# Loading one pair in bf16 on another queue, holding the next one back, and reordering the first stages of a fused attention and gated feed-forward kernel

## The chip, the cores and the metric

The kernel runs on one core of a Trainium2 chip. A core has a matrix engine (TensorE, PE in the profile, with its weight loads as PEld), VectorE (DVE), ScalarE (ACT), GpSimd (POOL) and SyncE (SP). SP, ScalarE and GpSimd can also issue DMAs. The time is the device time of one execution in microseconds; a kernel is judged by the median of several executions. The profile comes from one of them.

## The reference

The first half is attention with a relative position bias in the manner of T5, for 8 batches of 8 heads, 576 positions and a head size of 64. The second half is a bilinear feed-forward layer on the 4608 rows that come out.

```python
scores = scale * np.matmul(q, k.transpose(0, 1, 3, 2))
bias = bias_table[bucket]                     # bucket depends on |i - j| alone
scores = scores + bias.transpose(2, 0, 1)[None, :, :, :]
scores = scores - np.max(scores, axis=-1, keepdims=True)
attn = np.exp(scores)
attn = attn / (np.sum(attn, axis=-1, keepdims=True) + 1e-09)
attn_out = np.matmul(attn, v)                 # (8, 8, 576, 64)
...
x = attn_out.transpose(0, 2, 1, 3).reshape(B * S, H * D)
a = x @ w_a                                   # 512 -> 1536
b = x @ w_b
out = (a * b) @ w_out                         # 1536 -> 512
```

All inputs and the output are float32 in DRAM; the weights are 512 x 1536 (twice) and 1536 x 512.

## The kernel before

**Pairs.** Two heads of one batch make a pair; pair p is heads 2(p mod 4) and the next of batch p div 4, so there are 32 pairs, and pairs 0 to 3 are batch 0. Of the 576 positions 512 are the main part (four blocks of 128) and 64 are the tail. For each pair TensorE needs q and k with the head size on the partitions: `QT` and `KT`, two buffers each, which also hold the transposed tails. The names of the steps are those of small functions. `qk1(p, t)` makes the scores of key block t, `ex` is ScalarE's exponential, `mul` is VectorE's product with the exponential of the bias (`W_sb[p % 4]`, a band around the diagonal), `qk_tail`, `ex_tail` and `mul_tail` do the same for what touches the tails (with `Wt_sb`), `av(p, jq)` multiplies with v for query block jq, `norm` divides by the row sums and writes `XG`, and `t_x` turns `XG` into the feed-forward input `xn_sb`, by a DMA transpose on SP for most pairs, or on TensorE with a copy `c_x` for pairs 2 and 3.

**Loads.** q, k and v are read in rows of 64 floats (256 bytes). Loads issued on GpSimd cast to bf16 as they move (`load_p`, `load_t`, `load_vp`, `load_tails`, `load_vt`); loads on SP and ScalarE keep float32 (`load32`, into `q32`, `k32` and, for the tails of batch 0, `qt32`, `kt32`). Before the change all four pairs of batch 0 come in float32 on SP, with k of pair 0 on ScalarE, and are turned by float32 transposes (`t32`, against `id32`). From batch 1 on, q and k come through GpSimd into `qn`, `kn` (two buffers, by batch), v into `vm` (main) and `vt` (tails), the tails of q and k into `qtl`, `ktl` (a buffer for two batches). Pairs 4 to 11 are turned on TensorE in bf16 (`t_q`, `t_k`, with `c_q`, `c_k` as copies out of PSUM), later ones by DMA transposes.

**The bias table.** A small float32 matmul with a one-hot matrix makes the 8 x 256 table, ScalarE takes its exponential, and it goes out to a DRAM tensor `tab`. The bands `W_sb` and `Wt_sb` are read back from it with overlapping rows (`load_w`, and the loop over hh at L225), on GpSimd. `warm_up(n)` puts n products of zeros on TensorE before and after the table's matmul.

**Order.** Every engine's order is that of the program text; nothing is scheduled by a planner. So is the order of each DMA queue. On GpSimd, eight semaphores go round over its DMAs, so an issue waits until the one eight places before it has landed; SP's and ScalarE's DMAs share another eight. After the start, GpSimd's order is: W of pair 0, Wt, v of pair 0 and its tails, W of pair 1, the rest of v of batch 0, W of pair 2, q and k of pair 4, W of pair 3, the tails of batch 1, the first third of w_a and w_b, v of pair 4, the tails of v of batch 1, the rest of q and k of batch 1, the second third of w_a and w_b, the rest of v of batch 1, the last third, then q and k of batch 2, w_out (`wo_sb`), memsets of the second tail buffers, and the tails of q and k of batches 2 and 3.

**Stages.** A loop over s = 0, 1, 2 does pairs 0 to 2 with `q_next`, `k_next` and `tails_next` for the pair after; straight code does pair 3 and begins pair 4 and the feed-forward. From s = 4 on each stage does one pair and between its steps puts feed-forward units (`U`): for each chunk of 512 rows 12 units `ff_a` (x @ w_a, `pa`, copied to `ha`), 12 `ff_b` (`pb`, whose product with `ha` is `g`), and 12 thirds of `ff_o` (`po`, g @ w_out). The first chunk's 24 units of a and b are used up in stage s = 7, where the first `ff_o` stands on TensorE just behind `t_k(8)`, the transposes of k of pair 8 with its tails.

```python
        for mc in range(m0, m1):
            nc.tensor.matmul(out=ff[key][:, :], lhsT=w[df // FW][:, mc, 128 * (df % FW):128 * (df % FW) + 128],
                             rhs=xn_sb[mc][:, xin(c)],
                             start=(mc == 0), stop=(mc == NMC - 1))
```

`xn_sb[mc]` is filled by pair mc of the batch, so the first unit of each kind is begun with mc 0 to 2 and ended with mc 3 (`m0 = 3`) once pair 3 is there.

Of the kernel before, what the change touches and what calls it, by code (L numbers as in the profile page):

```python
# [13 lines left out]
def kernel(  # L14
# [11 lines left out]
    nc = tc.nc  # L26
    FP32 = mybir.dt.float32
    BF16 = mybir.dt.bfloat16
# [6 lines left out]
    SM = 128 * NM  # L35
# [6 lines left out]
    NMC = DM // 128  # L42
# [107 lines left out]
    def load_tails(b, nb):  # L150
        load_pad(nc.gpsimd, k, ktl[b // 2 % 2], b, nb)
        load_pad(nc.gpsimd, q, qtl[b // 2 % 2], b, nb)

    def load_vt(b, nb):
        load_pad(nc.gpsimd, v, vt[b // 2 % 2], b, nb)

    def load_w_in(part):
        for src, dst in ((moe_w_a, wa_sb), (moe_w_b, wb_sb)):
            nc.gpsimd.dma_start(
                out=dst[part][:, :, :],  # L160
                in_=src[:, WC * part:WC * part + WC].rearrange("(m p) n -> p m n", p=128))

    def load_w_out():
        nc.gpsimd.dma_start(out=wo_sb[:, :, :], in_=moe_w_out.rearrange("(t p) n -> p t n", p=128))

    def load_w(eng, hp):
        eng.dma_start(out=W_sb[hp][:, :, :],
                      in_=bass.AP(tensor=tab, offset=2 * hp * TB, ap=[[1, 128], [TB, 2], [1, 384]]))
# [12 lines left out]
    def load32(p, src, out, engs):  # L181
        for h in range(2):
            load_h(engs[h], src, out[:, p, :, h, :], 0, 2 * p + h)
# [18 lines left out]
    ones(nc.gpsimd, vt[0])  # L202
    for x in (ktl, qtl):
        pad(nc.gpsimd, x[0], Dh)
    for p in (2, 3):
        load32(p, q, q32, (nc.sync, nc.sync))
        load32(p, k, k32, (nc.sync, nc.sync))

    warm = ps_ff.tile([128, 512], FP32, tag="ffn", name="warm")

    def warm_up(n):
        for _ in range(n):
            nc.tensor.matmul(out=warm[:, :], lhsT=zero_sb[:, 0:128], rhs=zero_sb[:, :],
                             start=True, stop=True)
# [2 lines left out]
    tps = ps_av.tile([128, 512], FP32, tag="av", name="tab_ps")  # L217
    nc.tensor.matmul(out=tps[0:H, 0:NR], lhsT=bt_sb[0:NB, :], rhs=oh_sb[0:NB, :],
                     start=True, stop=True)
    warm_up(5)  # L220
    nc.scalar.activation(out=tab_sb[0:H, 127:127 + NR], in_=tps[0:H, 0:NR], func=ACTF.Exp)
    nc.scalar.dma_start(out=tab.ap(), in_=tab_sb[0:H, :])

    load_w(nc.gpsimd, 0)
    for hh in range(2):  # L225
        nc.gpsimd.dma_start(out=Wt_sb[64 * hh:64 * hh + 64, :, :],
                            in_=bass.AP(tensor=tab, offset=hh * TB + 192,
                                        ap=[[1, 64], [2 * TB, H // 2], [1, 192]]))
    load_vp(0, 0)
    load_vt(0, 1)  # L230
    load_w(nc.gpsimd, 1)
    load_t(v, None, 0, 2, 8)
    load_w(nc.gpsimd, 2)
    load_p(q, qn, 1, 0)
    load_p(k, kn, 1, 0)
    load_w(nc.gpsimd, 3)
    load_tails(1, 1)
    load_w_in(0)
    load_vp(1, 0)
    load_vt(1, 1)  # L240
    load_t(q, qn, 1, 2, 8)
    load_t(k, kn, 1, 2, 8)
    load_w_in(1)
# [4 lines left out]
    def copy(eng, out, in_):  # L248
        if eng is nc.scalar:
            nc.scalar.activation(out=out, in_=in_, func=ACTF.Copy)  # L250
        else:
            nc.vector.tensor_copy(out=out, in_=in_)
# [21 lines left out]
    def bank(where, dt, name):  # L274
        return where[0].tile([128, 512 if dt is FP32 else 1024], dt, tag=where[1], name=name)
# [212 lines left out]
    def ff_bank(name):  # L488
# [4 lines left out]
            where = TR if turn3 % 3 == 0 else FF  # L493
        return where[0].tile([128, 512], FP32, tag=where[1], name=name)

    def ff_mm(c, df, w, key, m0, m1):
        if m0 == 0:
            ff[key] = ff_bank(f"{key}{c}_{df}")
        for mc in range(m0, m1):
            nc.tensor.matmul(out=ff[key][:, :], lhsT=w[df // FW][:, mc, 128 * (df % FW):128 * (df % FW) + 128],  # L500
                             rhs=xn_sb[mc][:, xin(c)],
                             start=(mc == 0), stop=(mc == NMC - 1))

    def ff_a(c, df, m0=0):
        ff_mm(c, df, wa_sb, "pa", m0, NMC)
# [26 lines left out]
    units = []  # L532
    for c in range(NCH):
        for df in range(NDF):
            m0 = 3 if c == 0 and df == 0 else 0
            units.append(lambda c=c, df=df, m0=m0: ff_a(c, df, m0))
            units.append(lambda c=c, df=df, m0=m0: ff_b(c, df, m0))
        for tt in range(4):
            for part in range(3):
                units.append(lambda c=c, tt=tt, part=part: ff_o(c, tt, part))  # L540
# [9 lines left out]
    def t32(ps, src, p, t):  # L550
        nc.tensor.transpose(ps[:, 128 * t:128 * t + 128], src[:, p, t, :, :], id32[:, :])
# [13 lines left out]
    qk1(0, 1)  # L565

    def q_next(s):
        ps = bank(TR, FP32, f"trq{s + 1}")
        for t in range(NM):
            t32(ps, q32, s + 1, t)  # L570
        copy(None, QT[(s + 1) % 2][:, :], ps[:, :])

    def k_next(s):
        ps = bank(FF, FP32, f"trk{s + 1}")
        for t in range(NM):
            t32(ps, k32, s + 1, t)
        copy(None, KT[(s + 1) % 2][:, 0:SM], ps[:, :])

    def tails_next(p0, n, eng):
        ps = bank(FF, FP32, f"trt{p0}")  # L580
# [6 lines left out]
    for s in range(3):  # L587
        ex(s, 0)
        if s > 0:
            mul(s - 1, 3)  # L590
            mul_tail(s - 1)
        q_next(s)
        qk1(s, 2)
        ex(s, 1)
        k_next(s)
        qk1(s, 3)
        ex(s, 2)
        if s == 0:
            tails_next(0, 2, None)
        else:  # L600
            tails_next(s + 1, 1, ACT)
        if s > 0:
            av(s - 1, 0)
            av(s - 1, 1)
        qk_tail(s)
        mul(s, 0)
        mul(s, 1)
        ex(s, 3)
        if s > 0:
            av(s - 1, 2)  # L610
            norm(s - 1, 0)
            av(s - 1, 3, FF)
        qk1(s + 1, 0)
        ex_tail(s)
        if s > 0:
            av(s - 1, 4)
        mul(s, 2)
        if s > 0:
            norm(s - 1, 3)
            t_x(s - 1)  # L620
        qk1(s + 1, 1)

    load_w_in(2)
    load_t(q, qn, 2, 0, 8)
    load_t(k, kn, 2, 0, 8)
    load_w_out()
    pad(nc.gpsimd, vt[1], Dh + 1)
    ones(nc.gpsimd, vt[1])
    for x in (ktl, qtl):
        pad(nc.gpsimd, x[1], Dh)  # L630
    load_tails(2, 2)

    ex(3, 0)
    mul(2, 3)
# [18 lines left out]
    av_part(3, 0)  # L653
    c_x(2)
    t_q(4, FF)
    c_q(4)
    t_k(4, FF)
    c_k(4)
    qk1(4, 0)
    mul(3, 2)  # L660
    ex(4, 0)
# [2 lines left out]
    av_part(3, 2)  # L664
    av_part(3, None)
    mul(3, 3)
    qk1(4, 1)
    av_part(3, 3)
    ff_mm(0, 0, wa_sb, "pa", 0, 3)
    norm(3, 0)  # L670
    ex(4, 1)
    norm(3, 3)
    t_x(3, AV, range(3))
    ff_mm(0, 0, wb_sb, "pb", 0, 3)
    qk1(4, 2)
    t_x(3, AV, range(3, 5))
    ex(4, 2)
    c_x(3)
    qk1(4, 3)
# [101 lines left out]
```

## Time and profile before

| | us |
|---|---|
| median of 4 runs (lowest, highest) | 436.61 (435.23, 437.3) |
| profiled execution, its own time | 435.23 |
| its span | 433.4 |
| TensorE busy in the span | 413.7 (95%) |
| ScalarE, VectorE, GpSimd busy | 241.8, 196.9, 116.2 |
| mean granted clock of TensorE | 0.987 |

The span runs from the first to the last instruction of the profiled execution; 1.8 us of its time lie around it. A busy TensorE is not one at its peak, since matmuls are pipelined. Times on the timeline count from the span's start. A line of the timeline has the start, the duration, the engine, the line of the kernel, the operation, the tiles written and read, the shape, the number of instructions merged and, in brackets, how long the engine stood idle before and what ended that. A DMA issue on GpSimd shows the time of issuing, not of moving; the list of DMA issues has the time from issue to landing. "DMA share" is the mean busy share of the 16 DMA engines; it goes over 1 where several packets are under way in one engine.

### The profile page before, as it was taken

The numbers are of one execution on the slowest core, as the hardware profiler recorded it, in microseconds if no ns is written. First come the engines' busy times: TensorE is split into PE (matmuls) and PEld (weight loads), VectorE is DVE, ScalarE is ACT, GpSimd is POOL, SyncE is SP. The second block draws the span as 40 slices with busy tenths as digits, with TensorE's granted clock in tenths as the row PEclk, the third lists the DMA queues.
The fourth block names the chain that finished last, engine by engine and source line by source line (L and its number), as shares of the span: only waits on it lengthen the run. The fifth ranks groups of instructions, "written<-read, shape, count | busy, mean of one in ns | idle before, by whom it ended". The sixth has DMA issues, their size and how long they took to land.

```text
span 433.4 us, 8391 instructions
## 1 busy us (share of the span) xinstructions
PE 413.7 (95%) x3365; PEld 203.6 (47%) x3365; DVE 196.9 (45%) x474; ACT 241.8 (56%) x341; POOL 116.2 (27%) x155
## 2 busy tenths in 40 slices
PE   8697997699999999999999999999999999999995
PEld 3464553255444444444444444444444454444442
DVE  3585664145663455335542555355524550430330
ACT  3695566266665666666656666566657642323321
POOL 5895756830626400560037002100000000000000
PEclk9899999699999999999999999999999999999999
DMA  8999999997999990699339920931021012002004
GB/s 161 185 145 129 168 169 188 139 141 172 82 93 76 200 145 15 48 190 156 54 29 188 176 41 8 185 82 39 15 86 39 15 17 81 17 2 97 2 0 97
DMA packets 168279, 41.93 MB, mean 97 GB/s; under 512 B 158728, under 2 KB 163408, under 8 KB 168240
## 3 DMA queue, kind: packets, MB, share of 16 engines
q0 software_dynamic: 108400, 18.69, 60.9%
q1 hardware_dynamic: 58576, 22.38, 27.1%
q8 instruction: 26, 0.43, 0.4%
q10 hardware_dynamic: 1264, 0.34, 0.4%
q14 instruction: 13, 0.11, 0.1%
HBM read 38.80 MB, written 9.45 MB: 111 GB/s over the span
## 4 chain that ended last, share of the span: by engine, by line
PE 80%; DMA 13%; POOL 4%; issue 1%; ACTq 0%; DVE 0%; ACT 0%
PE po L519 22%; PE pa L500 20%; PE pb L500 19%; PE av L404 7%; PE qk L334 6%; DMA vm<-in_v_dram 4%; DMA qn<-in_q_dram 3%; PE av L395 3%; DMA qtl<-in_q_dram 2%; DMA wa<-in_moe_w_a_dram 2%; PE qkt L359 1%; PE qkt L362 1%; DMA k<-in_k_dram 1%; DMA bias_tab<-tab_sb 1%; POOL kn L124 1%
## 5 line engine op out<-in xcount | busy, mean ns | idle before, releaser
L345 ACT ACTIVATE at<-qk 128x1024 bf16<-128x1024 f32 x128 | 126.3, 1025 | 26.4 <-PE qk L334 26.4
L512 DVE TENSOR_TENSOR g<-pb,ha 128x512 bf16<-128x512 f32 x108 | 74.7, 692 | 114.4 <-PE pb L500 96.0
L500 PE MATMUL pa<-xn,wa 128*128 128x512 bf16 x432 | 111.4, 379 | 1.3 <-DMA xn<-XG 0.8
L500 PE MATMUL pb<-xn,wb 128*128 128x512 bf16 x432 | 111.2, 379 | 0.0
L519 PE MATMUL po<-wo,g 128*128 128x512 bf16 x432 | 103.8, 383 | 0.0
L507 ACT ACTIVATE ha<-pa 128x512 f32<-128x512 f32 x108 | 64.6, 598 | 67.5 <-PE pa L500 67.5
L353 DVE TENSOR_TENSOR at<-at,W 128x512 bf16<-128x512 bf16 (+1 forms) x128 | 60.1, 483 | 11.7 <-ACT at L345 8.4
L500 PEld LDWEIGHTS <-wa 128*128 128x128 bf16 x432 | 38.9, 98 | 49.6 <-issue 10.0
L523 ACT ACTIVATE ob<-po 128x512 f32<-128x512 f32 x36 | 21.5, 597 | 70.3 <-PE po L519 70.3
L519 PEld LDWEIGHTS <-g 128*128 128x128 bf16 x432 | 38.9, 99 | 46.4 <-issue 8.5
L500 PEld LDWEIGHTS <-wb 128*128 128x128 bf16 x432 | 39.0, 98 | 45.2 <-issue 5.6
L124 POOL DMA_DIRECT2D vm<-in_v_dram x32 | 27.8, 891 | 108.8 <-PE av L404 102.5
L404 PE MATMUL av<-vm,at 128*128 128x65 bf16 x992 | 44.8, 195 | 0.0
L404 PEld LDWEIGHTS <-at 128*128 128x128 bf16 x992 | 40.6, 99 | 4.1
L440 DVE RECIPROCAL rc<-av 128x6 f32<-128x6 f32 x64 | 12.1, 188 | 59.9 <-PE av L404 57.6
L395 PE MATMUL av<-vt,att 128*128 128x130 bf16 x156 | 35.2, 226 | 2.4 <-DMA vt<-in_v_dram 2.0
L373 ACT ACTIVATE att<-qkt 128x1024 bf16<-128x1024 f32 x32 | 32.7, 1022 | 0.0
L441 DVE TENSOR_TENSOR XG<-av,rc 128x384 bf16<-128x384 f32 x64 | 31.4, 491 | 2.2
L124 POOL DMA_DIRECT2D qn<-in_q_dram x28 | 24.7, 918 | 25.6 <-PE trq L286 19.2
L124 POOL DMA_DIRECT2D kn<-in_k_dram x28 | 24.7, 917 | 7.7 <-DMA vt<-in_v_dram 2.9
L334 PE MATMUL qk<-QTb,KTb 64*128 64x512 bf16 x160 | 24.2, 381 | 0.0
L395 PEld LDWEIGHTS <-att 128*128 128x128 bf16 x156 | 15.4, 98 | 18.0 <-DVE XG L441 10.7
(105 smaller groups left out, 229.2 us busy)
## 6 DMA issues: line engine op xcount, KB each, us to landing
out_dram<-ob SPq DMA_DIRECT2D x32, 256.0 KB, 3.1
qn<-in_q_dram POOLq DMA_DIRECT2D x24, 128.0 KB, 8.5
kn<-in_k_dram POOLq DMA_DIRECT2D x24, 128.0 KB, 11.8
vm<-in_v_dram POOLq DMA_DIRECT2D x24, 128.0 KB, 5.7
wa<-in_moe_w_a_dram POOLq DMA_DIRECT2D x3, 512.0 KB, 6.8
wb<-in_moe_w_b_dram POOLq DMA_DIRECT2D x3, 512.0 KB, 9.6
wo<-in_moe_w_out_dram POOLq DMA_DIRECT2D x1, 1536.0 KB, 14.5
q<-in_q_dram SPq DMA_DIRECT2D x8, 128.0 KB, 3.7
```

Source lines behind the costliest of these rows:

```text
L124: nc.gpsimd.dma_start(out=(vm[b % 2][:, h0:h1, t, 0:Dh] if dst is None else dst[b % 2][:, :].rearrange("p (t h d) -> p t h d", h=H, t=NM)[ ...
L334: nc.tensor.matmul(out=ps[:, hh, :], lhsT=kT_(p, t)[r, :], rhs=qT[r, :, :], start=True, stop=True)
L345: nc.scalar.activation(out=at[:, :, :], in_=ps[:, :, :], func=ACTF.Exp, scale=scale)
L353: nc.vector.tensor_tensor(out=at[:, :, lo:hi], in0=at[:, :, lo:hi], in1=w[:, :, y:(None if z < 0 else z):-1], op=MULT)
L373: nc.scalar.activation(out=at[:, 0:1024].rearrange("p (a x) -> p a x", a=2), in_=ps[:, :, :], func=ACTF.Exp, scale=scale)
L395: nc.tensor.matmul(out=pav[:, slot, :, :], lhsT=x, rhs=vt[b // 2 % 2][:, 4 * i + hp, :, 0:Dh + 1], start=fresh, stop=True, skip_group_chec ...
L404: nc.tensor.matmul(out=pav[:, slot, hh, :], lhsT=x, rhs=vm[i][:, 2 * hp + hh, t, 0:Dh + 1], start=False, stop=True, skip_group_check=True)
L441: nc.vector.tensor_tensor(out=xg[:, j0:j0 + n, :, :], in0=pav[:, 0:n, :, 0:Dh], in1=rc.unsqueeze(3).to_broadcast([128, n, 2, Dh]), op=MULT)
L500: nc.tensor.matmul(out=ff[key][:, :], lhsT=w[df // FW][:, mc, 128 * (df % FW):128 * (df % FW) + 128], rhs=xn_sb[mc][:, xin(c)], start=(mc ...
L507: nc.scalar.activation(out=ha[:, :], in_=ff["pa"][:, :], func=ACTF.Copy)
L512: nc.vector.tensor_tensor(out=g_sb[df][:, :], in0=ff["pb"][:, :], in1=ff["ha"][:, :], op=MULT)
L519: nc.tensor.matmul(out=po[:, :], lhsT=g_sb[df][:, 128 * tt:128 * tt + 128], rhs=wo_sb[:, df, :], start=(df == 0), stop=(df == NDF - 1))
```

## The change

- Pair 2's q and k no longer come in float32 on SP but by `load_p` into `qn[0]` and `kn[0]`, in bf16, on GpSimd, at the place where SP's loads of pairs 2 and 3 stood in the text. That is before the first `load_w` in GpSimd's order. `q_next` and `k_next` turn them in bf16 for s = 1.
- Pair 3's four float32 loads stay on SP but are written down inside stage s = 0, and two one-element memsets on VectorE, behind `mul(0, 0)`, write into the same buffers first, so the loads wait for these.
- `Wt` is loaded on SP instead of GpSimd. The second `warm_up` has 2 products instead of 5.
- The tails of v of batches 0 and 1 are loaded together. The tails of q and k of batch 1 go behind the first third of w_a and w_b.
- The memsets and the tails of q and k of batches 2 and 3 go ahead of q and k of batch 2 and of w_out.
- In the stages s = 1 and 2, `qk_tail(s)` and `mul(s, 0)` go ahead of `av(s - 1, 0)`; `av(s - 1, 2)` and `norm(s - 1, 0)` come ahead of `mul(s, 1)`, and `norm(s - 1, 3)` and `t_x(s - 1)` ahead of `mul(s, 2)`.
- Pair 4's copies out of PSUM move to ScalarE, both behind both transposes. `av_part(3, 3)` goes ahead of `qk1(4, 1)`.
- The feed-forward sums run over mc in the order 0, 2, 1, 3, and the first units are begun with two terms instead of three; the second of them a little later.

```diff
-    for p in (2, 3):
-        load32(p, q, q32, (nc.sync, nc.sync))
-        load32(p, k, k32, (nc.sync, nc.sync))
+    load_p(q, qn, 0, 2)
+    load_p(k, kn, 0, 2)
...
-    warm_up(5)
+    warm_up(2)
     nc.scalar.activation(out=tab_sb[0:H, 127:127 + NR], in_=tps[0:H, 0:NR], func=ACTF.Exp)
     nc.scalar.dma_start(out=tab.ap(), in_=tab_sb[0:H, :])
 
     load_w(nc.gpsimd, 0)
     for hh in range(2):
-        nc.gpsimd.dma_start(out=Wt_sb[64 * hh:64 * hh + 64, :, :],
+        nc.sync.dma_start(out=Wt_sb[64 * hh:64 * hh + 64, :, :],
...
     load_vp(0, 0)
-    load_vt(0, 1)
+    load_vt(0, 2)
...
     load_w(nc.gpsimd, 3)
+    load_w_in(0)
     load_tails(1, 1)
-    load_w_in(0)
     load_vp(1, 0)
-    load_vt(1, 1)
...
+    MC = (0, 2, 1, 3)
+
...
-        for mc in range(m0, m1):
+        for i in range(m0, m1):
+            mc = MC[i]
...
-                             start=(mc == 0), stop=(mc == NMC - 1))
+                             start=(i == 0), stop=(i == NMC - 1))
...
-            m0 = 3 if c == 0 and df == 0 else 0
+            m0 = 2 if c == 0 and df == 0 else 0
...
     def q_next(s):
-        ps = bank(TR, FP32, f"trq{s + 1}")
+        ps = bank(TR, BF16 if s == 1 else FP32, f"trq{s + 1}")
         for t in range(NM):
-            t32(ps, q32, s + 1, t)
-        copy(None, QT[(s + 1) % 2][:, :], ps[:, :])
+            if s == 1:
+                nc.tensor.transpose(ps[:, 128 * t:128 * t + 128], blocks(qn, 2)[:, t, :, :], ident)
+            else:
+                t32(ps, q32, s + 1, t)
+        copy(None, QT[(s + 1) % 2][:, :], ps[:, 0:SM])
...
-        if s > 0:
+        qk_tail(s)
+        mul(s, 0)
+        if s == 0:
+            nc.vector.memset(q32[0:1, 3, 0, 0, 0:1], 0.0)
+            nc.vector.memset(k32[0:1, 3, 0, 0, 0:1], 0.0)
+            load32(3, q, q32, (nc.sync, nc.sync))
+            load32(3, k, k32, (nc.sync, nc.sync))
+        else:
             av(s - 1, 0)
             av(s - 1, 1)
-        qk_tail(s)
-        mul(s, 0)
+            av(s - 1, 2)
+            norm(s - 1, 0)
         mul(s, 1)
         ex(s, 3)
         if s > 0:
-            av(s - 1, 2)
-            norm(s - 1, 0)
             av(s - 1, 3, FF)
         qk1(s + 1, 0)
         ex_tail(s)
         if s > 0:
             av(s - 1, 4)
-        mul(s, 2)
-        if s > 0:
             norm(s - 1, 3)
             t_x(s - 1)
+        mul(s, 2)
         qk1(s + 1, 1)
 
     load_w_in(2)
-    load_t(q, qn, 2, 0, 8)
-    load_t(k, kn, 2, 0, 8)
-    load_w_out()
     pad(nc.gpsimd, vt[1], Dh + 1)
     ones(nc.gpsimd, vt[1])
     for x in (ktl, qtl):
         pad(nc.gpsimd, x[1], Dh)
     load_tails(2, 2)
+    load_t(q, qn, 2, 0, 8)
+    load_t(k, kn, 2, 0, 8)
+    load_w_out()
...
     t_q(4, FF)
-    c_q(4)
     t_k(4, FF)
-    c_k(4)
+    c_q(4, ACT)
+    c_k(4, ACT)
...
     mul(3, 3)
+    av_part(3, 3)
     qk1(4, 1)
-    av_part(3, 3)
-    ff_mm(0, 0, wa_sb, "pa", 0, 3)
+    ff_mm(0, 0, wa_sb, "pa", 0, 2)
     norm(3, 0)
     ex(4, 1)
     norm(3, 3)
     t_x(3, AV, range(3))
-    ff_mm(0, 0, wb_sb, "pb", 0, 3)
     qk1(4, 2)
     t_x(3, AV, range(3, 5))
+    ff_mm(0, 0, wb_sb, "pb", 0, 2)
```

`k_next` is changed in the same way as `q_next`.

More of the change, by code (lines that the diff above doesn't have):

```diff
@@ L567, in q_next @@
     def q_next(s):
-        ps = bank(TR, FP32, f"trq{s + 1}")
+        ps = bank(TR, BF16 if s == 1 else FP32, f"trq{s + 1}")
         for t in range(NM):
-            t32(ps, q32, s + 1, t)
-        copy(None, QT[(s + 1) % 2][:, :], ps[:, :])
+            if s == 1:
[3 more added lines that the diff above has]
+        copy(None, QT[(s + 1) % 2][:, :], ps[:, 0:SM])
     def k_next(s):
-        ps = bank(FF, FP32, f"trk{s + 1}")
+        ps = bank(FF, BF16 if s == 1 else FP32, f"trk{s + 1}")
         for t in range(NM):
-            t32(ps, k32, s + 1, t)
-        copy(None, KT[(s + 1) % 2][:, 0:SM], ps[:, :])
+            if s == 1:
+                nc.tensor.transpose(ps[:, 128 * t:128 * t + 128], blocks(kn, 2)[:, t, :, :], ident)
+            else:
+                t32(ps, k32, s + 1, t)
+        copy(None, KT[(s + 1) % 2][:, 0:SM], ps[:, 0:SM])
     def tails_next(p0, n, eng):
@@ L601 @@
             tails_next(s + 1, 1, ACT)
-        if s > 0:
+        qk_tail(s)
[5 more added lines that the diff above has]
+            load32(3, k, k32, (nc.sync, nc.sync))
+        else:
             av(s - 1, 0)
             av(s - 1, 1)
-        qk_tail(s)
-        mul(s, 0)
+            av(s - 1, 2)
+            norm(s - 1, 0)
         mul(s, 1)
```

## The prediction

> **What bounds the kernel now.** I read the page's slices first, then the waits of TensorE, then the timeline where the longest wait lies, and last the chain of work with the DMA issues around it. The slices:
>
> ```profile
> span 433.4 us, 8391 instructions
> PE   8697997699999999999999999999999999999995
> PEclk9899999699999999999999999999999999999999
> DMA  8999999997999990699339920931021012002004
> ```
>
> One digit is 10.8 us. From the ninth slice (87 us) TensorE is full, whatever the DMA engines do; before it they are full in every slice but the first, and TensorE is not. Only the first 87 us can give time back. The waits of TensorE in the first 100 us (total, times, longest):
>
> ```profile
> PE trk L298 <- DMA ktl<-in_k_dram: 5.5, 1, 5.5
> PE av L395 <- DMA vt<-in_v_dram: 2.0, 1, 2.0
> PE qk L334 <- DVE KT L252: 1.4, 2, 0.9
> ...
> PE trk L298 <- DMA qtl<-in_q_dram: 0.9, 1, 0.9
> ```
>
> The 6.4 us on the tails of batch 2 (ktl, qtl) are one stretch, here on the timeline of TensorE:
>
> ```profile
> 72.97 0.39 PE L306 MATMUL trk<-cst_sb,kn 128*128 128x128 bf16 x4
> 78.88 0.26 PE L298 MATMUL trk<-cst_sb,ktl 128*128 128x128 bf16 x1 [5.52 <-DMA ktl<-in_k_dram]
> 80.01 0.27 PE L298 MATMUL trk<-cst_sb,qtl 128*128 128x128 bf16 x1 [0.87 <-DMA qtl<-in_q_dram]
> 80.07 1.91 PE L519 MATMUL po<-wo,g 128*128 128x512 bf16 x4
> ```
>
> What TensorE does next, at 80.07, is the first output product, and it reads wo. The DMAs issued from 62.4 to 70 us (KB each, us from issue to landing), and the chain of work there (start, us):
>
> ```profile
> wo<-in_moe_w_out_dram POOLq DMA_DIRECT2D x1, 1536.0 KB, 14.5
> ktl<-in_k_dram POOLq DMA_DIRECT2D x2, 64.0 KB, 10.9
> qtl<-in_q_dram POOLq DMA_DIRECT2D x2, 64.0 KB, 10.8
> ```
>
> ```profile
> 48.84 13.40 DMA qn<-in_q_dram
> ...
> 62.52 1.02 POOL wo L164
> ...
> 69.22 10.71 DMA qtl<-in_q_dram
> 79.92 0.09 issue
> ```
>
> wo lands at 62.52 + 14.5 = 77.0, the last tail at 69.22 + 10.71 = 79.9, although it is only 64 KB: GpSimd's DMAs come in the order of issue, and each landing is the sum of what was queued before. So the bound up to 80 us is the transfer work in GpSimd's queue, and four tails take 79.9 - 77.0 = 2.9 us of it.
>
> **The change, part by part.** (1) Tails first. They now go ahead of q and k of batch 2 and of wo. The 5.5 and 0.9 us are gone; late next is wo. With the same transfers in another order, wo lands where the last tail did: 77.0 + 2.9 = 79.9. TensorE comes to po at 72.97 + 0.39 plus two transposes (0.27 each), 73.9, and stands still until then. Behind po in its order stand the tail scores of pair 7, and behind these ScalarE's tail exps and VectorE, as they stand behind the tails today (ScalarE 9.1 us). By order alone the change is worth 80.07 - 80.0 = 0.1 us.
>
> The memsets (63.58 to 67.26, 3.7 us) and the issues of the tails (2.7 us) stand on GpSimd ahead of q and k of batch 2; those eight issues waited 0.8 + 1.6 + 0.8 + 2.7 us for earlier landings, and their loads land 11.9 us after issue, so the queue does not run dry. Without that cover this would cost up to 6.4 us. q and k land 2.9 us later: the last kn at 60.11 + 8.7 = 68.8 goes to 71.7, before 72.97. Their buffers are now read by pair 2's transposes too, some 30 us before, which delays nothing.
>
> (2) Pair 2. Four SP loads in f32 go, four casting loads enter GpSimd's queue at 4.44 us, ahead of the first W. A pair of such issues takes 1.53 us (19.72), so four end at 7.5, under the wait for the bias table to 8.87. Their transfer work, by stage (engine columns, clock, DMA share, GB/s at the end):
>
> ```profile
> 5.00:7.00 2.00, 2.00 (x7) 0.98 (x6) 0.00 (x0) 0.00 (x1) 0.00 (x0) 1.00 1.33 226
> 7.00:8.00 1.00, 1.00 (x7) 1.00 (x6) 0.35 (x2) 0.38 (x1) 0.00 (x0) 1.00 0.98 153
> 8.00:9.00 1.00, 0.97 (x5) 0.25 (x3) 0.78 (x2) 0.00 (x0) 0.13 (x1) 1.00 0.52 112
> 9.00:11.00 2.00, 1.80 (x12) 1.03 (x12) 0.83 (x2) 1.98 (x3) 2.00 (x4) 1.00 0.87 198
> ```
>
> At 226 GB/s a load of 128 KB in f32 takes 0.58 us, four 2.3; casting loads ran at 149 GB/s (60 to 62 us, nothing else moving), so 64 KB of bf16 take 0.44, four 1.8. That saves 0.5 us. And against a share of 1.33, the stretch from 7 to 11 us has 0.26 + 0.61 + 0.69 = 1.6 us unused, which the new loads fall into. Bounds of the saving: none (a cast row costs an f32 row, and taking pair 2 from 9 to 14 us opens as much idle time as it fills), or all of it, 2.3 + 1.6 = 3.9. I take 0.5 plus two thirds of 1.6, 1.5 us: between 9 and 14 us some of the opened time must stay empty, because GpSimd issues a 64 KB load every 0.8 us and its transfer takes 0.44.
>
> The Trainium skill ("DMA: Bandwidth & Descriptors", section "Issuing engines are not separate DMA queues") speaks against this part: DMAs of all issuing engines run on the same 16 DMA engines, and a second issuer saves only issue time. By that rule the saving is the 0.5 us at most and the time 436.0.
>
> (3) Pair 3 held back, Wt on SP. Two memsets (0.09 us each, as at 3.31) follow mul(0,0) at 14.05 on VectorE; SP's four loads start behind them, about 14.5 instead of 10.06. Behind SP's waits for the bias table and for this stand only the transposes of XG, from 23.8. The loads of 9.5 to 11.7 landed after 6.0 to 7.5 us, so now 20.5 to 23.7; their users stood at 23.34 and 24.25. Cost between -1 and +1.5 us at that place. GpSimd loses the two Wt issues (1.29 us), so vm, vt and W follow sooner by about that.
>
> (4) Order in the pairs, warm-ups, bf16 transposes, ScalarE's copies, first units. qk_tail(1) no longer stands behind the 2.0 us wait for vt, which now costs ScalarE 2.92 us before 21.26. Four bf16 transposes take 0.39 against 0.66 us, their copy 0.42 against 0.68. Three warm-ups less are 1.3 us, though the first transpose cannot start before k lands at 2.22 + 3.9 = 6.1 and starts at 6.21; a clock that rises later could cost half of the 3.4 us for which it stayed low after 18.97. ScalarE's two copies cost about 0.6 each (by the ha row, 598 ns) where it idles 1.84. The unit order changes which of xn is read first and removes at most the 0.83 us wait for xn at 37.31. The tails of batch 1 go behind wa and wb; the latter lands at 26.55 + 9.6 = 36.2, the tails up to 1.6 later, and they are due at 39.99. Together between 5 us gained and 4 lost before 41 us, and at the end nothing: a gain meets pair 5's last kn, which lands at 40.98 + 4.5 = 45.5 less the 1.5 saved, right when its transposes stand (45.27); a loss is covered by TensorE's wait for wo, 78.4 - 73.9 = 4.5 us.
>
> (5) The clock. From 80.05 to 83.82 TensorE ran at a granted 0.50, which costs half of 3.77, 1.9 us. After a wait of some 5 us it should do so again; ends: none of it, or 3.4 us, if a low stretch is nearly doubled. I take no difference.
>
> Sum: po starts at 77.0 + 2.9 - 1.5 + 0.1 = 78.5 instead of 80.07, so 1.6 us less. What follows keeps its order and amount, so the end moves by the same. The profiled execution took 435.23 (span 433.4 and 1.8 around it) and would take 433.6; it was the lowest of four, 1.4 below the median of 436.61, so against that: **435.0 us**.
>
> **Rivals.** Order only: the saving is 0 to 0.7 us; for it, the DMA slices are full of nines and work is conserved; against it, the share of 0.52 at 8 us. Time 436.5. More saved: the loads of pair 2 hide wholly, and W and the first v no longer share the engines with SP's f32 loads; W took 5.1 us to land at 8.87 with little ahead of it. Saving 2.4 to 3.9, middle 3.2, time 433.3. The wait vanishes: wo is in place when po comes; then 6.4 us and the 1.9 of clock go, 428.3. Against it, wo took 8.2 us (68.8 to 77.0) in a full queue. The skill's fit in the same page, "Anatomy of one DMA — SWDGE (gpsimd) path", about 2.0 us plus bytes over 436 GB/s, would give 5.6 us from issue and this case; the row says 14.5.
>
> Slower: the bias table lands late. Its write took 3.4 us (5.16 to 8.57) beside SP's loads alone; now four more loads compete. The DMAs issued from 9.4 to 14 us, with both queues at work, took 5.7 to 6.8 us. At 6.5 the table lands at 11.7, GpSimd stands still 3.1 us longer, the DMA engines run empty meanwhile, and only the 0.5 remains: wo at 77.0 + 2.9 - 0.5 + 3.1 = 82.5, po at 82.6, 2.5 us lost, 439.1. It decides from a table at 10.2 us, whose delay of 1.6 equals the whole gain.
>
> **How the numbers follow.** Forecast (0.7 to 2.4 us saved, own range 434.2 to 435.9) 0.42; order only 0.20; more saved 0.20; wait vanishes 0.05; table late 0.13. What a measurement here can tell from no change is 0.5%, 2.2 us: 434.4 to 438.8. Faster: 0.12 of the forecast, 0.20 and 0.05, 0.37. Slower: 0.11 of the last. The rest, 0.52, is the same. The range reaches from 431.5 to 438.0, leaving out the vanished wait and most of the late table.
>
> **What would show it.** Right: no wait for ktl or qtl near 73 us, and in its place one of po for wo of 4 to 7 us that ends near 78.5, with a clock of 0.50 behind it; pair 5's transposes still at kn's landing, near 44; W issued near 8.9. Wrong: TensorE full through 70 to 80 us; W issued after 10; a wait over 4.5 us before 41 us; or wo landing before 76 or after 80.

## The result and the profile after

The changed kernel takes 435.54 us in the median of 45 executions (429.98 to 439.49), the kernel before, on the same chips, 436.51 in 71 (434.19 to 438.98). The ratio is 0.9958, 95% interval 0.9946 to 0.9971: 1.8 us less, 0.4%. The ratio, here and below, leaves out executions more than 1.5% above their kernel's fastest, six of the 45 (436.45 to 439.49) and none of the 71, so it favours the kernel that varies more; the medians, of all executions, are 0.97 us apart. The gain is thus 1.0 to 1.8 us, within what the prediction called no change (0.5%), and the median lies beside its 435.0 us.

The profiled execution took 435.5 us, with a span of 433.7; before's took 435.23 and 433.4. So this pair of executions does not show the gain, and its landings cannot be subtracted from each other to find it. What it shows is which wait took the place of which. The slices of the page, and the waits of TensorE in the first 100 us (total, times, longest):

```profile
span 433.7 us, 8393 instructions
...
PE   7889897599999999999999999999999999999995
...
PEclk9999999699999999999999999999999999999999
DMA  9999999997999991699239940931021002002004
```

```profile
PE po L520 <- DMA wo<-in_moe_w_out_dram: 7.1, 1, 7.1
PE trk L552 <- DMA k<-in_k_dram: 1.5, 1, 1.5
...
PE trk0a L552 <- DMA k<-in_k_dram: 1.1, 1, 1.1
PE trk L304 <- DMA kn<-in_k_dram: 1.1, 2, 0.7
```

From the ninth slice on TensorE is full as before, and its low seventh and eighth slices are still there. The waits for `ktl`, `qtl` and `vt` are gone. In their place stand one of 7.1 us of `po` for `wo`, and one of 1.5 for k of pair 3. On the timeline of TensorE:

```profile
73.10 0.39 PE L304 MATMUL trk<-cst_sb,kn 128*128 128x128 bf16 x4
73.32 0.22 PE L296 MATMUL trk<-cst_sb,ktl 128*128 128x128 bf16 x1
73.38 0.22 PE L296 MATMUL trk<-cst_sb,qtl 128*128 128x128 bf16 x1
80.66 1.89 PE L520 MATMUL po<-wo,g 128*128 128x512 bf16 x4 [7.06 <-DMA wo<-in_moe_w_out_dram]
```

The tails are there when TensorE comes to them at 73.32, it stands still from 73.60, and `po` starts at 80.66, where it had started at 80.07. The chain of work (start, duration) ends there on one transfer:

```profile
66.67 13.94 DMA wo<-in_moe_w_out_dram
80.61 0.05 issue
80.66 1.46 PE po L520 x3
```

At the start the queue of GpSimd moved, too. Its timeline before and after, at the first `W`, in brackets the time that it stood still for the bias table:

```profile
8.87 0.85 POOL L167 DMA_DIRECT2D W<-bias_tab  x1 [4.43 <-DMA bias_tab<-tab_sb]
```

```profile
10.20 0.72 POOL L167 DMA_DIRECT2D W<-bias_tab  x1 [2.68 <-DMA bias_tab<-tab_sb]
10.90 1.52 POOL L130 DMA_DIRECT2D vm<-in_v_dram  x2
```

And the windows from 9 to 20 us (window, five engines, granted clock, DMA share, GB/s), before and after:

```profile
9.00:20.00 11.00, 7.38 (x60) 4.51 (x61) 5.57 (x13) 8.89 (x11) 9.75 (x14) 0.95 1.36 190
```

```profile
9.00:20.00 11.00, 8.91 (x82) 5.04 (x82) 5.91 (x16) 9.28 (x13) 9.80 (x14) 1.00 1.22 132
```

The first `W` is issued 1.3 us later, and in the eleven microseconds behind it the DMA engines move 132 GB/s instead of 190. These two lines are what the experiments below are mostly about.

### The profile page after: what moved, and what is told of

It is laid out like the page before. It is cut to its first block, busy times and chain, and to the rows that moved or that the text cites. A ratio compares the mean times of both kernels' runs of the same rounds, so it can differ in the third digit from the quotient of the medians.

```text
span 433.7 us, 8393 instructions
## 1 busy us (share of the span) xinstructions
PE 411.5 (95%) x3362; PEld 201.4 (46%) x3362; DVE 195.7 (45%) x474; ACT 243.2 (56%) x343; POOL 116.8 (27%) x155
## 4 chain that ended last, share of the span: by engine, by line
PE 84%; DMA 10%; POOL 3%; issue 1%; DVE 0%; ACTq 0%; ACT 0%; POOLq 0%
PE po L520 22%; PE pa L501 21%; PE pb L501 20%; PE av L402 8%; PE qk L332 6%; DMA wo<-in_moe_w_out_dram 3%; PE av L393 3%; DMA wb<-in_moe_w_b_dram 2%; DMA vm<-in_v_dram 2%; PE qkt L357 1%; PE qkt L360 1%; DMA kn<-in_k_dram 1%; DMA bias_tab<-tab_sb 1%; DMA k<-in_k_dram 1%; POOL kn L124 1%
## 5 line engine op out<-in xcount | busy, mean ns | idle before, releaser
L402 PE MATMUL av<-vm,at 128*128 128x65 bf16 x992 | 43.8, 193 | 0.4 <-DVE at L351 0.4
L402 PEld LDWEIGHTS <-at 128*128 128x128 bf16 x992 | 39.6, 97 | 4.7 <-DVE at L351 0.5
```

The source lines that it names most:

```text
L402: nc.tensor.matmul(out=pav[:, slot, hh, :], lhsT=x, rhs=vm[i][:, 2 * hp + hh, t, 0:Dh + 1], start=False, stop=True, skip_group_check=True)
```

## The experiments

Theory: until about 80 us the time is set by the transfers in GpSimd's queue, whose end TensorE awaits at `po`; the change only names another last transfer, and gains what the early loads save. First rival: the gain is in the order of the last transfers, and the early edits give nothing. Second rival: the wait for `wo` is not the price, so that TensorE would stand still elsewhere without it. In the ten profiles that keep the place of `po` and one load of `wo`, the span ends 352.9 to 354.3 us after `po` starts, so there the start of `po` is the number to read; with later output products or `wo` in thirds (349.7 to 357.1) it is not. Times of landings and starts are those of one profile each.

**Tails first, alone.** Before, with only the order of the last transfers changed:

```diff
     load_w_in(2)
-    load_t(q, qn, 2, 0, 8)
-    load_t(k, kn, 2, 0, 8)
-    load_w_out()
     pad(nc.gpsimd, vt[1], Dh + 1)
...
     load_tails(2, 2)
+    load_t(q, qn, 2, 0, 8)
+    load_t(k, kn, 2, 0, 8)
+    load_w_out()
```

> The kernel before with one edit: the memsets and the tails of batches 2 and 3 go ahead of q and k of batch 2 and of w_out. Theory A (the sum of GpSimd's transfers decides, and w_out takes the place of the tails as what lands last): the waits for ktl and qtl (6.4 us) go, a wait of po for wo of 6 to 7 us comes, ending within 0.7 us of 80; time -0.7 to +0.7 us against before. Theory B (the tails' wait was the loss, and w_out is only a little late): po starts before 78 us and the time falls by 1.5 us or more; then this edit alone gives the measured gain of 1.8 us.

Measured: 435.66 us in the median of 12, ratio 0.9970 (0.9949 to 0.9992), 1.3 us less. Its waits of TensorE:

```profile
PE po L519 <- DMA wo<-in_moe_w_out_dram: 6.2, 1, 6.2
PE av L395 <- DMA vt<-in_v_dram: 2.5, 1, 2.5
```

The wait for the tails is turned into one for `wo` here too, of the same size, but `wo` lands at 78.84 and `po` starts at 78.89 (this execution, 433.9, is the second fastest of the twelve). The time lies between the two theories. The order alone is worth most of what the whole change is by the ratios, 1.3 of 1.8 us, and all of it by the medians, 0.97 us each.

**Tails last, in the changed kernel.** The reverse edit in the kernel after.

```diff
     load_w_in(2)
+    load_t(q, qn, 2, 0, 8)
+    load_t(k, kn, 2, 0, 8)
+    load_w_out()
     pad(nc.gpsimd, vt[1], Dh + 1)
...
     load_tails(2, 2)
-    load_t(q, qn, 2, 0, 8)
-    load_t(k, kn, 2, 0, 8)
-    load_w_out()
```

> The changed kernel with its order of GpSimd's last loads put back: q and k of batch 2, w_out, then memsets and tails. Theory A: the last of the same transfers lands at the same moment; TensorE waits for ktl and qtl instead of wo and goes on within 0.7 us of where the changed kernel does; time within 0.7 us of the changed kernel's, so 1.1 to 2.5 us below before by the ratio. Theory B: the wait for the tails comes on top, and the time is 1.5 us or more above the changed kernel's.

Measured: 436.85 us in the median of 12, ratio 0.9969 (0.9932 to 1.0006). Its executions lie between 430.89 and 440.22, the median is 0.2 us above before's 436.63, and the interval holds no change as well as 3 us gained: inconclusive on the early edits. The profile, one of the longer executions (437.83), shows the old wait back:

```profile
81.58 0.27 PE L296 MATMUL trk<-cst_sb,ktl 128*128 128x128 bf16 x1 [7.20 <-DMA ktl<-in_k_dram]
82.63 0.27 PE L296 MATMUL trk<-cst_sb,qtl 128*128 128x128 bf16 x1 [0.79 <-DMA qtl<-in_q_dram]
82.69 1.91 PE L520 MATMUL po<-wo,g 128*128 128x512 bf16 x4
```

Here `wo` landed at 78.89 and the last tail 3.65 us later.

**Later output products.** The changed kernel with fewer feed-forward units in stages 6 to 8, so that TensorE comes to `po` later and with other work done before it:

```diff
-    quotas = {4: 6, 5: 7, 6: 7, 7: 7, 8: 6}
+    quotas = {4: 6, 5: 7, 6: 6, 7: 4, 8: 2}
```

> The changed kernel with fewer feed-forward units in stages 6 to 8 (quotas 6, 7, 6, 4, 2 instead of 6, 7, 7, 7, 6), so that the first output product comes in the middle of stage 8 instead of stage 7, by then with w_out landed; the units left out there are done at the end. Theory A (the wait for w_out is idle time of TensorE at the end of the only stretch that is bound by transfers): the 7.1 us wait shrinks to under 2 us, a wait of about 1 us for kn comes at the transposes of pair 8, the low clock behind the wait goes; time 5 to 8 us below before. Theory B (TensorE would only wait elsewhere, for q, k or v of batch 2 or ScalarE): less than 2 us below the changed kernel.

The same edit on before with its tails first:

> The kernel before with the tails of batch 2 first and the smaller quotas of stages 6 to 8, and nothing else of the change. Theory D (the early edits, pair 2 in bf16 and pair 3 held back, win nothing that reaches the end; moving the tails did it all): as fast as the changed kernel with the smaller quotas, ratio 0.984 to 0.991 to before, 431 to 432.5 us. Theory E (the early edits save transfer time as the forecast has it, 1.5 us): 1 to 2 us slower than that, 432.5 to 433.5 us.

Measured: 431.27 us in the median of 6, ratio 0.9873 (0.984 to 0.9906), and 432.83, ratio 0.9903 (0.9881 to 0.9926). TensorE around `po` in the first:

```profile
79.94 0.38 PE L304 MATMUL trk<-cst_sb,kn 128*128 128x128 bf16 x4 [0.52 <-DVE QT L250]
80.16 0.22 PE L296 MATMUL trk<-cst_sb,ktl 128*128 128x128 bf16 x1
80.22 0.22 PE L296 MATMUL trk<-cst_sb,qtl 128*128 128x128 bf16 x1
80.28 1.02 PE L520 MATMUL po<-wo,g 128*128 128x512 bf16 x3
```

`wo` lands at 80.24, as late as ever, and nobody waits for it. With the wait go 5.5 us from the kernel before (0.0127 of 436.6), and the granted clock stays at 1.00 behind it. So the wait for `wo` had a price, and the rival that TensorE would stand elsewhere holds in part: 4.3 us came back as time (435.54 to 431.27) of the 7.1 waited. From 60 to 100 us TensorE's waits come to 4.0 us instead of 7.3, the new ones all short (1.1 us for `vt` at 85.5 is the longest). The half-speed stretch behind `po`, 2.87 us of work in the kernel after, is gone too, an estimated 1.4 us; 3.3 and 1.4 are about the 4.3. By median this is the fastest version, though the intervals of the other three near it overlap with its own. The second kernel has none of the early edits and the same `po` at 80.30 without a wait; what the rest of the change adds here is the 0.3% between the two ratios, whose intervals overlap.

**w_out in thirds.** The changed kernel with three DMAs in the place of one:

```diff
-        nc.gpsimd.dma_start(out=wo_sb[:, :, :], in_=moe_w_out.rearrange("(t p) n -> p t n", p=128))
+        for i in range(0, NDF, 4):
+            nc.gpsimd.dma_start(out=wo_sb[:, i:i + 4, :],
+                                in_=moe_w_out[128 * i:128 * i + 512, :].rearrange("(t p) n -> p t n", p=128))
```

> The changed kernel with w_out loaded by three DMAs of a third each, in the same place of GpSimd's queue. If it is the landing of the one large DMA that TensorE waits for: the first third lands 5 to 5.5 us before the last, po starts near 75, and the 7.1 us wait splits into one of about 1.5 us and two of 1 to 2.5 us ahead of the second and third part; the work between them (8 products and pair 7's tail scores) and a clock that need not fall save 2 to 4 us against the changed kernel. If TensorE comes too late to profit, or the two extra issues delay the rest: within 0.7 us.

Measured: 432.56 us in the median of 6, ratio 0.991 (0.9888 to 0.9931).

```profile
74.06 1.04 PE L522 MATMUL po<-wo,g 128*128 128x512 bf16 x4 [1.44 <-DMA wo<-in_moe_w_out_dram]
...
76.95 1.02 PE L522 MATMUL po<-wo,g 128*128 128x512 bf16 x4 [1.35 <-DMA wo<-in_moe_w_out_dram]
80.12 1.20 PE L522 MATMUL po<-wo,g 128*128 128x512 bf16 x4 [2.14 <-DMA wo<-in_moe_w_out_dram]
```

The last third lands at 80.07, no sooner than the whole did. But the first unit needs the first third alone, and while the next ones land, TensorE does the work that had stood behind: it stands still 4.9 us in three parts instead of 7.1 in one. That is a second way to the same end: the transfers are as they were, what TensorE does meanwhile is not.

**Pair 2 in bf16, alone.** Before, with the loads of pair 2 on GpSimd ahead of `W`, and the bf16 transposes that they need; pair 3 stays at once on SP, `Wt` on GpSimd, the tails last:

```diff
-    for p in (2, 3):
-        load32(p, q, q32, (nc.sync, nc.sync))
-        load32(p, k, k32, (nc.sync, nc.sync))
+    load_p(q, qn, 0, 2)
+    load_p(k, kn, 0, 2)
+    load32(3, q, q32, (nc.sync, nc.sync))
+    load32(3, k, k32, (nc.sync, nc.sync))
```

> The kernel before with pair 2's q and k loaded by GpSimd in bf16 ahead of W, turned in bf16, and nothing else; pair 3 is loaded by SP at once. By the forecast's working (0.5 us of transfer and part of the idle share from 7 to 11 us): pair 5's last kn lands 1 to 1.5 us earlier and the last tail too, the time falls by 1 to 2 us. If the four loads cost the bias table what they save: W is issued 0.5 to 1.3 us later than the 8.65 to 8.87 of before, time within 0.7 us of before.

Measured: 435.79 us in the median of 12, ratio 0.9972 (0.9949 to 0.9995), 1.2 us less. The profile has `W` at 10.18, 1.3 us late, and `po` at 80.63, no sooner than before:

```profile
10.18 0.72 POOL L167 DMA_DIRECT2D W<-bias_tab  x1 [2.66 <-DMA bias_tab<-tab_sb]
```

So the timed executions show a small gain that this one profile does not.

**Pair 2 behind the first W.** The changed kernel, where the loads of pair 2 do not go under the wait for the bias table:

```diff
-    load_p(q, qn, 0, 2)
-    load_p(k, kn, 0, 2)
...
     load_w(nc.gpsimd, 0)
+    load_p(q, qn, 0, 2)
+    load_p(k, kn, 0, 2)
```

> The changed kernel with pair 2's four loads behind the first W in GpSimd's order. In the changed kernel's profile the bias table is written out at 5.83 and W issued at 10.20, against 5.16 and 8.87 before. Theory C (the four loads delay the table and with it all of GpSimd's queue): the table lands by 8.9, W is issued by 9.0, but pair 2's transfers now come behind it; w_out lands within 1 us of the changed kernel's, time within 1 us. If the loads did not delay the table (it varies by itself): W is issued near 10 here too, and the time is 1 to 2 us above the changed kernel's, because the early idle share of the DMA engines is not used.

Measured: 436.95 us in the median of 12, ratio 1.0007 (0.9986 to 1.0028). The intervals of this and of the kernel after are apart: the place ahead of `W` is worth 2.1 us by the ratios (0.0049 of 436.5) and 1.4 by the medians, and without it the whole change gives nothing. GpSimd's timeline:

```profile
8.94 0.83 POOL L167 DMA_DIRECT2D W<-bias_tab  x1 [4.49 <-DMA bias_tab<-tab_sb]
9.77 1.53 POOL L130 DMA_DIRECT2D qn<-in_q_dram  x2
11.26 1.52 POOL L130 DMA_DIRECT2D kn<-in_k_dram  x2
12.73 1.53 POOL L130 DMA_DIRECT2D vm<-in_v_dram  x2
14.19 1.45 POOL L146 DMA_DIRECT2D vt<-in_v_dram  x2
15.56 0.81 POOL L167 DMA_DIRECT2D W<-bias_tab  x1
```

Two things are seen at once. `W` is back at 8.94, as in all five profiles with no loads ahead of it (8.65 to 8.94). And the four issues behind it cost GpSimd 3.0 us, so that the second `W` follows 6.6 us behind the first, where after has 3.55 (10.20 to 13.75): time to issue looks scarce here, and under the wait for the table GpSimd only stands.

**No holding back of pair 3.** The changed kernel with pair 3's loads at once on SP, without the memsets:

```diff
     load_p(q, qn, 0, 2)
     load_p(k, kn, 0, 2)
+    load32(3, q, q32, (nc.sync, nc.sync))
+    load32(3, k, k32, (nc.sync, nc.sync))
...
-        if s == 0:
-            nc.vector.memset(q32[0:1, 3, 0, 0, 0:1], 0.0)
-            nc.vector.memset(k32[0:1, 3, 0, 0, 0:1], 0.0)
-            load32(3, q, q32, (nc.sync, nc.sync))
-            load32(3, k, k32, (nc.sync, nc.sync))
-        else:
+        if s > 0:
```

> The changed kernel with pair 3's float32 loads not held back: no memsets, the loads stand on SP ahead of Wt. In the profiles, from 9 to 20 us the DMA engines move 116 to 136 GB/s in the changed kernel against 183 to 198 before. Theory F (pair 2's move saved its share, but holding pair 3 back opened an idle stretch of the same size): 170 GB/s or more from 9 to 20 us, pair 5's last kn and w_out land 1 to 2 us earlier, the time is 1 to 2 us below the changed kernel's. Theory G (the held loads only make room for W and v, which decide): W and v land later, pair 5's last kn where it was, time within 0.7 us or above.

Measured: 434.0 us in the median of 12 (431.17 to 436.08), ratio 0.9942 (0.9918 to 0.9966), against 435.54 and 0.9958 for the kernel after. The intervals overlap, so the times alone do not settle what the holding back costs; 0.7 us by the ratios, 1.5 by the medians. The profile, at 431.17 the fastest of the twelve, in windows and waits:

```profile
9.00:20.00 11.00, 9.80 (x45) 4.82 (x46) 5.32 (x13) 7.84 (x9) 10.81 (x15) 1.00 1.79 194
```

```profile
PE po L522 <- DMA wo<-in_moe_w_out_dram: 3.2, 1, 3.2
...
PE trk0a L554 <- DMA k<-in_k_dram: 1.0, 1, 1.0
```

The DMA engines are full again between 9 and 20 us, 194 GB/s, and no wait for k of pair 3 is left. `wo` lands at 75.97. Not all of the 132 GB/s of the kernel after is the hold's: pair 2 alone, without the hold and with `W` late (10.18), has 162 in this window, and the later products, with the hold and `W` early (8.79), have 156. The same with the later output products:

> The changed kernel with pair 3 not held back and with the smaller quotas of stages 6 to 8: the two edits that each helped. If the transfer time saved by not holding pair 3 back is worth something once no wait for w_out is left (pair 5's kn and the loads of batch 2 come earlier, so the waits before 60 us shrink): 429.5 to 430.7 us, 1 us or more below the changed kernel with the smaller quotas alone (431.27). If both edits remove the same wait: within 0.7 us of 431.27. Either way the fastest so far or level with it.

Measured: 431.91 us in the median of 6, ratio 0.9895 (0.9869 to 0.9922), level with 0.9873 with the hold. `wo` lands at 77.89, `po` starts at 77.93 and waits for nothing. So once no one waits for the end of the queue, no price of the hold is seen in the times. That fits the reading that the hold costs time at the end of the queue, but does not show it: in this profile, the fastest of the six (429.55), TensorE's waits before 60 us come to 6.4 us, in that with the hold (431.78) to 9.3.

**Repeats.** The kernel before, and the kernel after twice, unedited, to see how far one profile stands for others.

> The kernel before once more, for a second profile: how far the landing of pair 5's last kn (45.5), of w_out (77.0) and of the last tail (79.9) vary by themselves. If by 1 us or more, a single profile does not tell a saving of 1.5 us.

> The changed kernel once more, unedited, for a second profile of it. The kernels with pair 2's loads ahead of the first W spread more widely (standard deviation 1.85 us over 45 executions here, 0.84 with these loads behind W), and their profiles have the first W issued anywhere from 8.8 to 11.0 us. Theory (the landing of the bias table sets the time of each execution): a profile with W issued by 9.3 has po start by 78.0 and a time under 433.5, one with W issued after 10.0 has po at 80 to 82.6 and 435 to 438. Rival (the spread arises later, in the full queue): no such order, for instance W before 9.3 with po after 80, or W after 10.0 with po before 78.

> The same once more, for a third profile. Theory: W issued by 9.3 goes with po by 78.0 and a time under 433.5; W issued after 10.0 goes with po at 80 to 82.6 and 435 to 438; each 1 us of delay of W is about 1 us at po. Rival: the landing of wo doesn't follow the issue of W.

Measured: before 434.7 us, with `W` at 8.79 and `po` at 80.03; `wo` and the last tail land at 76.89 and 79.89, within 0.15 us of the first profile, pair 5's last kn at 44.46, 1.0 us sooner. After 435.99, with `W` at 10.44 and `po` at 79.87; and 437.17, with `W` at 10.88 and `po` at 81.42:

```profile
PE po L520 <- DMA wo<-in_moe_w_out_dram: 6.0, 1, 6.0
PE trk L552 <- DMA k<-in_k_dram: 2.9, 1, 2.9
PE trk0a L552 <- DMA k<-in_k_dram: 1.5, 1, 1.5
```

These waits are of the last one. In all three profiles of the kernel after, `W` goes out after 10 us. The theory stated there does not hold: the execution with the later `W` (10.44 against 10.20) has the earlier `po`, and 79.87 lies just outside the band of 80 to 82.6. The early `W` that it asks for was caught with the later products, whose program is the same up to stage 6: `W` at 8.79, and yet `wo` lands at 80.24, not before 78. Over the five profiles with this start and this order of the queue `W` goes out from 8.79 to 10.88 and `wo` lands from 79.83 to 81.37, the earliest `W` in the middle. How late `W` is does not by itself set the end of the queue.

## Why the prediction came out

The sum was right, 1.6 us predicted and 1.0 (medians) to 1.8 (ratio) measured, and so was the wait: that for the tails becomes one for `wo`, and the end of GpSimd's queue decides. Where in the queue the gain comes from was not right: two terms were mis-sized, in opposite directions, and that they nearly cancel is luck.

**(1) Tails first: right on the wait, mis-sized on the order.** "By order alone the change is worth 80.07 - 80.0 = 0.1 us" rested on the assumption that the same transfers in another order take the same time. Measured alone it is 1.3 us (0.35 to 2.2). From the landing of the last third of w_b to that of the last of `wo` and the tails, the four profiles with the tails last took 20.0 to 20.8 us, the ten with the tails first 18.5 to 19.8, means 20.3 and 19.1. Counted from the issue of that third, the means are 33.3 and 32.5 and the groups overlap, so part of it is tails that now move beside w_b.

For the rest the traces have an account. The prediction took a landing for "the sum of what was queued before". But when the last tail lands, 9.75 and 9.76 MB of GpSimd's queue have moved since the span's start (before and its repeat); with the tails first alone, 9.53 and 9.58 when `wo` lands. The loads of v that stand behind the last tail move partly beside it, those behind `wo` less so. The 0.2 MB between them are some 1.3 us at the 152 GB/s of 77 to 80 us before, an estimate. Against it, a new slack stretch came: from 64.0 to 65.4 us the kernel after moves 37 GB/s, at a DMA share of 5.69, where before moves 152 at 2.94. Between the landings of w_b and `wo` all ten profiles with the tails first have 0.4 to 2.0 us under 60 GB/s (counted in steps of 0.2 us), the four others none. The prediction had that "the queue does not run dry" there; the share says that packets were under way, but what slows them stays open.

The rest of (1) held: `kn` of batch 2 is in place at 73.10 without a wait, though its loads go behind the memsets and the tails. `wo` was put at 79.9 by order alone and lands at 78.84 with order alone, at 80.26 with that order and later output products; in the kernel after, where 1.5 more should have come off, its three profiles have 79.83, 80.61 and 81.37.

**(2) Pair 2: the size fits only without the hold.** "1.5 us" was 0.5 for bf16 and two thirds of an idle 1.6. The kernel without the hold, set against tails first alone, has it: 434.0 against 435.66, 1.7 us by the medians and 1.2 by the ratios (0.9942, 0.9970), whose intervals overlap; it has `Wt` on SP and all of (4) besides. Pair 2 alone gave 1.2 (0.2 to 2.2). So the size fits, within a wide band. And the place under the wait counts, 1.4 to 2.1 us. The kernel after comes close to the lower bound that the prediction named, no saving, but with pair 3's hold in it.

**(3) Pair 3 held back: its price in the queue was left out.** It was costed "at that place", -1 to +1.5 us, and at the end at nothing. The place was as predicted: the loads go out from 15.10 and land at 21.08 to 23.85 ("20.5 to 23.7"), and TensorE waits 1.5 us for k at 24. What was overlooked is the queue: little else is ready to move in the time that the four loads leave. 132 GB/s from 9 to 20 us instead of 190, in part the hold and in part the late `W`, and by the profiles the lost time is still lost at `wo`. From the issue of the first `W` to the landing of `wo` the five profiles with pair 2 ahead of `W` and the hold (after, its repeats, later products, thirds) took 69.4 to 71.5 us, mean 70.4; the two without the hold 66.8 and 68.6, mean 67.7; and tails first alone, with pair 2 in float32, 70.2, or 71.5 with later products. So in the profiles the kernel without the hold is some 3 us shorter in this stretch, and the hold gives most of it back; this rests on two profiles, one of them the fastest of its twelve. Pair 2's loads are not all of the 3 us: alone, with the tails last, they took this stretch from 71.1 (before and its repeat, to the last tail) to 70.2. By the times the net of (2) and (3) is 0.1 (medians, 435.66 to 435.54) to 0.5 us (ratios) instead of 1.5. The prediction had the premise for this in its own part (2) and did not use it for (3). That the hold is what eats the gain is the likeliest reading, not a shown one: the intervals with and without it overlap.

**(4) Order in the pairs, warm-ups, copies, units: not resolved.** "At the end nothing" has no run of its own. The wait for `vt` went, and pair 5's transposes still stand at kn's landing, but at 45.85 and not "near 44". The kernel with pair 2 behind `W` has all of (4) and (1) and gains nothing, which speaks against a large gain in (4), though the hold and the issues behind `W` could hide one.

**(5) The clock: right, but for the early stretch.** Low from 76.70 to 83.53 after, 6.8 us, as from 77.00 to 83.82 before. Before, 3.77 us of work lay in it behind the start of `po`, now 2.87, a difference of 0.45 us in half speed. With later products the changed kernel has no such stretch, with and without the hold; the kernel before with tails first has one of 3.4 us, from 85.27. The other low stretch of before, 3.4 us from 18.97, is not in after's first profile (1.00 from 18.97 to 22.38), but nor is it in before's repeat, while after's last has one from 17.77: it comes and goes between executions of one kernel.

**The rivals.** "The bias table lands late" happened by its own sign: `W` at 10.20, 10.44 and 10.88 in the three profiles, at or past the 10.2 from which it should decide. By the prediction's own marks for wrong (`W` after 10, `wo` after 80) two of the three profiles are on that side, while the timed executions are not: its time, 439.1, lies 3.6 us above the median. The early `W` with later products, and `wo` at 80.24 all the same, speak against it as the account. "The wait vanishes" did not happen, and its price was too high: 428.3 was named, and taking the wait away gave 431.3, since TensorE stands still elsewhere for about half of it. The way there was the place of `po`, not the transfers. "More saved" is what the kernel without the hold leans to: its 434.0 lies between that rival's 433.3 and the forecast.

**What the skill's rules made of it.** The Trainium skill ("DMA: Bandwidth & Descriptors", section "Issuing engines are not separate DMA queues") was cited against (2): a second issuer saves issue time only. The runs agree in that 1.4 to 2.1 us hang on where in GpSimd's order four issues of 0.76 us stand; 0.5 us as the most was too little where issue time runs short. (0.5 off 436.6 is 436.1, not the 436.0 that the prediction has.) The page's fit in "Anatomy of one DMA — SWDGE (gpsimd) path", about 2.0 us and bytes over 436 GB/s, would give an estimate of 5.6 us for `wo`. It took 13.94, and its thirds, issued 0.7 us apart, landed 7.4, 9.6 and 12.0 us after their issues. The time from issue to landing is mostly the queue ahead.

## What to carry to other kernels

When a consumer waits for the end of one long DMA queue, do not stop at choosing which transfer comes last: look whether the consumer can come later, with other work put ahead of it (4.3 us on top of the change here, by the medians), or begin on a part of the transfer (3.0 us); both were worth more than all the reordering of loads (1.0 to 1.8 us). A transfer moved out of a busy stretch can gain only if something else is ready to fill the hole: read the GB/s of the stretch that it leaves, not only of the one that it enters. And where a change moves several loads, charge each of them to the end of the queue, not to the place of its first user.

## What the runs showed that was not expected

- The order of one large and four small transfers in one queue changed the time to the last landing by about 1.1 us (20.3 to 19.1, fourteen profiles, no overlap). With the small ones last, 0.2 MB of what was queued behind them had moved by then: a landing is not the sum of what stands ahead of it alone.
- Kernels with loads ahead of the bias table vary more: a standard deviation of 1.85 us over 45 executions of the kernel after, 2.65, 1.58 and 1.41 over 12 with the tails last, without the hold and with pair 2 alone, against 0.97 for before, 0.92 for tails first alone and 0.84 with these loads behind `W`. In their profiles the first `W` goes out anywhere from 8.79 to 10.96 us, in those of the other kernels from 8.65 to 8.94. Which of the competing loads decides it was not tried.
- The granted clock fell to 0.50 in the thirds version too, from 80.83 to 84.24, though no single standstill of TensorE there was longer than 2.1 us:

```profile
74.00:76.90 2.90, 1.53 (x11) 0.86 (x12) 0.45 (x3) 1.14 (x2) 0.69 (x1) 1.00 1.22 198
77.00:80.00 3.00, 0.98 (x4) 0.34 (x4) 0.20 (x2) 0.00 (x0) 0.88 (x1) 1.00 1.81 178
80.90:84.20 3.30, 3.30 (x15) 1.02 (x14) 0.00 (x0) 2.48 (x3) 3.21 (x5) 0.50 2.42 154
```

TensorE was busy for 0.98 of the 3.00 us from 77 to 80. The Trainium skill ("TensorE: Matmul & The Clock Gate", section "Part 1: The HAM clock gate (the "warmup" mystery)") describes windows of 3.4 us whose activity sets the clock, which fits the length of 3.41 us here and twice that after the long waits; every low stretch in the first 100 us of the fourteen profiles is 3.4 or 6.8 us long.
